# Low weight parts handed on from where they are made, conversions respread, rings of four

## The chip, the cores and the metric

The kernel runs on one core of one Trainium2 chip. The metric is the device time of one execution in microseconds (us). Engines: PE (TensorE), DVE (VectorE), ACT (ScalarE), POOL (GpSimd) and SP, whose queue issues nearly all DMAs. Each engine executes its own instructions in the order in which the program lists them.

## What is computed

Three stages run one after the other; all inputs are float32, but the two weights of the middle stage come to the chip as 64-bit floats.

```python
q_p, k_p = phi(q_s), phi(k_s)                 # attention with random features, 4 x 8 x 576 x 64
kv = einsum('bhsm,bhsd->bhmd', k_p, v);  z = sum(k_p, axis=2)
x = (einsum(q_p, kv) / (einsum(q_p, z) + 1e-6))       # -> 2304 tokens x 512
h = x @ w_in;  g = h / (1 + exp(-1.702 * h));  x = g @ w_out        # MLP, 512 -> 2048 -> 512
# top-1 mixture of 8 experts: out = gate * (relu(x @ w1[e]) @ w2[e]), e = argmax(x @ w_gate)
```

A float32 matmul operand is split in a high and a low part (`hi` rounded by a copy, `lo = x - hi`), and a product is made of three matmuls: high by high, high by low, low by high.

## The kernel before

**Attention.** The 18 tiles of 128 tokens run in a loop over `t` (L390), each iteration with a k tile five ahead and a q tile. `advance` (L319) issues the next load of a fixed sequence `k0 k1 .. k4 k5 q0 k6 q1 ..`; a k load (L200) is followed at once by the load of its v tile (L203), which goes into one of `NV = 5` tiles whose rows hold 65 floats for each head, 64 of them loaded (256 bytes at a time). Two `advance` calls later the tile is squared (L214), and then `proj` multiplies it (L231). `ksums` adds k and v (L257). Before the loop seven matmuls on a tile `warm` keep PE busy.

**MLP.** `steps` (L355) is a list of 80 pairs (block of tokens, f): block 0 with f = 0..7, block 1 with f = 0..15, block 0 with f = 8..15, then blocks 2, 3, 4. In loop iteration n (called step n here), PE does `hmm(n)` (12 matmuls, L439 to L441, with the weights `w_f`), and then `ymm(n-1)` (12 matmuls, L465, L466, L468, with the weights `o_f`). In between `gate(n)` runs on ACT (two gelus, L454 and L455) and DVE (L456). The tail of the attention lies in steps 0 and 1 by the table `DR`: in step 0 `num` and `norm` of the last tile follow `hmm(0)`, and in step 1 `xtr`, a transpose on PE (L308) and a copy on ACT (L309), follows `gate(1)`. After it the PSUM banks of the attention go to the MLP, so `ymm(0)`, at the end of step 1, waits for that copy.

**Conversion.** Each of the 32 weight chunks (`w_0..w_15`, `o_0..o_15`, 512 KB each) is loaded as 64-bit words into a staging tile (`cload`, L132) and turned into float32 by an absolute value on ACT (`cabs`, L139) and four DVE operations (`cops`, L117, L118, L120, L122); `chigh` copies the high part on ACT (L164), which stays in SBUF, and `clow` subtracts it (L172). The low part is stored to DRAM (`cstore`, L156), and every use of it, the first too, fetches it back (`wfetch`, L372, for step n+2; `ofetch`, L378, for step n+1). Low parts live in two rings, `l0` for w and `l1` for o, with three tiles each. The list `order` (L103) sets the order of the chunks: `w0 w1 o0 w2 o1 w3 o2 ..`. By the end of the attention eight chunks are done, with `clow` on POOL. The other 24 are done in the MLP, with `clow` on DVE: `CMLP = (2, 2, 2, 2, 2, 1)` is the number of conversions in steps 0 to 5, with one in each step after that. One "conversion" in the loop is `cabs(1)`, `cpop(4)`, `clow`, `chigh(1)`, `cload(1)` (L739 to L744), a software pipeline: the low part of a chunk is made one conversion after its high part. In the last four steps of each part of a block, `xsplit` (L359) splits the activations of the next part: a copy on ACT (L178) and a subtraction (L179) on DVE, or on POOL once all chunks are converted.

Of the kernel before, what the change touches and what calls it, by code (L numbers as in the profile page):

```python
# [10 lines left out]
F32 = mybir.dt.float32  # L11
F32R = mybir.dt.float32r
BF16 = mybir.dt.bfloat16
# [7 lines left out]
B, H, S, D, M = 4, 8, 576, 64, 128  # L21
NTOK, DM, DFF = 2304, 512, 2048
E, F = 8, 1024
NT = NTOK // 128
KC = DM // 128
NF = DFF // 128
# [3 lines left out]
NT0 = BLOCKS[-2][0]  # L30
# [10 lines left out]
NJ = NTOK // SUB  # L41
# [29 lines left out]
def fused_kernel(ctx: ExitStack, tc: tile.TileContext, qT, kT, vt, omT, w_in, w_out, w_gate, w_gateT, w1, w2, consts, out):  # L71
    nc = tc.nc
# [3 lines left out]
    wts = ctx.enter_context(tc.tile_pool(name="wts", bufs=1))  # L76
# [17 lines left out]
    def winc(f):  # L94
        return win[f // 4][:, f % 4]
# [4 lines left out]

    order = [0] + [c for f in range(NF - 1) for c in (f + 1, NF + f)] + [2 * NF - 1]  # L103
    cnext, cst2, cf32 = [0, 0, 0, 0, 0], [], {}
    for i in range(2):
        w = keep.tile([128, 2, 512, 2], I32, name=f"st{i}", tag=f"wg{i}", bufs=1)
        cst2 += [w[:, 0], w[:, 1]]

    def low(m):
        return wts.tile([128, 512], F32R, name=f"l{m}", tag=f"l{m}", bufs=3)  # L110

    def cops(i):
        t, lo, hi = cf32[i], cst2[i % 4][:, :, 0], cst2[i % 4][:, :, 1]
# [37 lines left out]
    halves, stored = [], []  # L151

    def cstore():

        for c, lo in stored:
            nc.sync.dma_start(out=lod[c], in_=lo.bitcast(F32))  # L156
        stored.clear()
# [10 lines left out]
    def clow(eng):  # L168

        for i, c, hi in halves:  # L170
            lo = low(int(c >= NF))
            eng.tensor_tensor(out=lo, in0=cf32.pop(i), in1=hi.bitcast(F32), op=ALU.subtract)  # L172
            stored.append((c, lo))
            cnext[4] += 1
        halves.clear()

    def split(hi, lo, src, eng):
        nc.scalar.copy(out=hi, in_=src)  # L178
# [5 lines left out]
    kp = kctx.enter_context(tc.tile_pool(name="attk", bufs=1, side="right"))  # L184
# [2 lines left out]
    wkp = qctx.enter_context(tc.tile_pool(name="attps", bufs=1, space=PSUM, side="left"))  # L187
    sp = sctx.enter_context(tc.tile_pool(name="atts", bufs=1, side="left"))
    omx = sp.tile([128, M], F32, name="omx", bufs=1)
    warm = kp.tile([128, 512], BF16, name="warm", bufs=1)  # L190

    NV = 5
    vs = [kp.tile([128, H, D + 1], F32, name=f"v{i}", tag=f"v{i}", bufs=1) for i in range(NV)]
    scale = 1.0 / np.sqrt(np.sqrt(D))
    raws = {}

    def load(kind, t):
        src = qT if kind == "q" else kT
        r = sp.tile([128, H, 128], F32, name="raw", tag="raw", bufs=4)
        nc.sync.dma_start(out=r[0:64].rearrange("p h t -> p (h t)"), in_=src[t])  # L200
        raws[kind, t] = r
        if kind == "k":
            nc.sync.dma_start(out=vs[t % NV][:, :, 0:D], in_=vt[t].rearrange("p (h d) -> p h d", h=H))  # L203


    SQ = (((nc.vector, 0, 4), (nc.scalar, 4, 8)), ((nc.scalar, 0, 8),), ((nc.gpsimd, 0, 6), (nc.vector, 6, 8)), ((nc.gpsimd, 0, 8),))
# [10 lines left out]
    pj, phi = {}, {}  # L217
# [27 lines left out]
    def kvacc(t, parts=(0, 1)):  # L245

        e, v = phi["k", t], vs[t % NV]
        for i, (r, n, b) in enumerate(segments(t)):
# [63 lines left out]
    seq = [("k", t) for t in range(LEAD)]  # L312
# [4 lines left out]
    ln = [0]  # L317

    def advance():  # L319
        if ln[0] < len(seq):  # L320
            load(*seq[ln[0]])
        if 2 <= ln[0] < len(seq) + 2:
            square(*seq[ln[0] - 2])
        ln[0] += 1
# [3 lines left out]
    for i in range(WARM):  # L328
        p = work_bank("wm")
# [22 lines left out]
    xsp, wsp, osp, phs, gsp, pys, ysb = {}, {}, {}, {}, {}, {}, {}  # L352
# [5 lines left out]
    def xsplit(v, k, eng):  # L358
        b = parts[v][0]  # L359
        n = BLOCKS[b][1] * 128  # L360
        xsp[b, k] = [xa.tile([128, 512], F32R, name=f"x{m}", tag=f"x{m}{(v * KC + k) % 6}", bufs=1)[:, 0:n] for m in "hl"]
        split(*xsp[b, k], xT[b][:, k], eng)

    def hilo(m):
        return [wts.tile([128, 512], F32R, name="wh1", tag="cf", bufs=3) if m else
                xb.tile([128, 512], F32R, name="wh0", tag="wh0", bufs=2), low(m)]

    def wfetch(b, f):

        lo = low(0)  # L370
        assert f in order[:cnext[4] - len(stored)]
        nc.sync.dma_start(out=lo.bitcast(F32), in_=lod[f])  # L372
        wsp[b, f] = winc(f).rearrange("p k f -> p (k f)"), lo

    def ofetch(b, f):
        lo = low(1)
        assert NF + f in order[:cnext[4] - len(stored)]
        nc.sync.dma_start(out=lo.bitcast(F32), in_=lod[NF + f])  # L378
        osp[b, f] = woutc(f), lo

# [9 lines left out]
    for t in range(NT):  # L390
        k = t + LEAD
        if t >= 2:
            norm(t - 2)
        if k < NT:
            proj("k", k)
            expo("k", k)
            advance()
        if t >= 1:
            qtr(t - 1)
        cpop(1)  # L400
        if k - 1 < NT:
            ksums(k - 1)
        if k == NT:
            kctx.close()
            xa = ctx.enter_context(tc.tile_pool(name="xa", bufs=1, side="right"))
            php = ctx.enter_context(tc.tile_pool(name="ph", bufs=1, space=PSUM, side="right"))
        proj("q", t)
        expo("q", t)
        cstore()
        cabs(1)  # L410
        clow(nc.gpsimd)
        advance()
        if k >= NT:
            advance()
        if t >= 1:
            num(t - 1)
        if t >= 2:
            xtr(t - 2)
        cpop(1)
        chigh(1)  # L420
        cload(1)
        for i in XSL.get(t, ()):
            xsplit(0, i, nc.gpsimd)
        if t >= NT - 3:
            (lambda: wfetch(0, 0), lambda: wfetch(0, 1), lambda: ofetch(0, 0))[t - NT + 3]()
    norm(NT - 2)
    sctx.close()


    xb = ctx.enter_context(tc.tile_pool(name="xb", bufs=1, side="right"))  # L430

    def hmm(b, f):
# [62 lines left out]
        del pys[b]  # L495

    def logit(b, j, e):
        junk = sb.tile([128, DM], F32, name="junk", tag="junk", bufs=1)
        t = BLOCKS[b][0] + j
        nc.vector.tensor_tensor_reduce(out=junk, in0=ysb[b][j], in1=wg[e // 4][:, e % 4], scale=1.0, scalar=0.0,  # L500
                                       op0=ALU.mult, op1=ALU.add, accum_out=lg[:, t, e:e + 1])
# [27 lines left out]
    def small(name, *shape):  # L529
        return sb.tile([128, *shape], F32, name=name, tag=name, bufs=1)  # L530
# [49 lines left out]
    def place(t0, nb):  # L580

        c = slice(t0, t0 + nb)
        v = small("pv", NT0, E)[:, 0:nb]
        jc = small("pj", NT0, NJ)[:, 0:nb]
        q = small("pq", NT0)[:, 0:nb]
        r = small("pr", NT0)[:, 0:nb]
        nc.vector.tensor_tensor(out=v, in0=oh[:, c], in1=bc(oh0, nb, 1), op=ALU.mult)
        nc.vector.tensor_reduce(out=inr[:, c], in_=v, axis=AX.X, op=ALU.add)

        nc.vector.scalar_tensor_tensor(out=q, in0=rank[:, c], scalar=n0[:, 0:1], in1=inr[:, c], op0=ALU.is_ge, op1=ALU.mult)  # L590
        nc.vector.scalar_tensor_tensor(out=r, in0=q, scalar=n0[:, 1:2], in1=rank[:, c], op0=ALU.mult, op1=ALU.add)

        nc.vector.tensor_tensor(out=inr[:, c], in0=q, in1=inr[:, c], op=ALU.subtract)
        nc.vector.tensor_scalar_add(inr[:, c], inr[:, c], 1.0)
        nc.vector.tensor_tensor(out=jc, in0=bc(r, NJ, 2), in1=bc(cst[:, C_J:C_J + NJ], nb, 1), op=ALU.is_ge)
        nc.vector.tensor_reduce(out=jf[:, c], in_=jc, axis=AX.X, op=ALU.add)
        nc.vector.tensor_scalar_add(jf[:, c], jf[:, c], -1.0)
        nc.vector.scalar_tensor_tensor(out=slot[:, c], in0=jf[:, c], scalar=-float(SUB), in1=r, op0=ALU.mult, op1=ALU.add)
# [80 lines left out]
    def esplit(i, f, m):  # L679
        spl[i, f, m] = hilo(m)  # L680
        split(*spl[i, f, m], ew[i % 2][f // 4 * 2 + m][:, f % 4 * 512:(f % 4 + 1) * 512], nc.vector)

    def drain(n, h):
        for c, t in DR.get((n, h), ()):
            dict(q=qtr, n=num, d=norm, x=xtr)[c](NT + t)
# [5 lines left out]
    for n in range(len(steps) + 1):  # L691
        if n < len(steps):
            b, f = steps[n]
            cstore()
            if n + 2 < len(steps):
                wfetch(*steps[n + 2])
            if n + 1 < len(steps):
                ofetch(*steps[n + 1])
            else:
                for m in range(2):  # L700
                    esplit(0, 0, m)
            drain(n, 0)
            hmm(b, f)
            gate(b, f)
            drain(n, 1)
            if n == 1:
                qctx.close()
                sb = ctx.enter_context(tc.tile_pool(name="sb", bufs=1, side="left"))
                ps = ctx.enter_context(tc.tile_pool(name="ps", bufs=1, space=PSUM, side="left"))
                wgT = sb.tile([128, KC, E], F32, name="wgT", bufs=1)  # L710
                lg = sb.tile([128, NT, E], F32, name="lg", bufs=1)
                mx = sb.tile([128, NT], F32, name="mx", bufs=1)
# [25 lines left out]
            if cnext[4] < len(order):  # L738
                for i in range(CMLP[n] if n < len(CMLP) else 1):  # L739
                    cabs(1)  # L740
# [4 lines left out]
            if (b, f) == (0, HF):  # L745
                assert cnext[4] == len(order)
                for i in range(2):
                    wg.append(keep.tile([128, 4, DM], F32, name=f"wg{i}", tag=f"wg{i}", bufs=1))
                    nc.sync.dma_start(out=wg[i].rearrange("p e d -> p (e d)"),
                                      in_=w_gate[4 * i:4 * i + 4].rearrange("(o e) d -> o (e d)", o=1).to_broadcast([128, 4 * DM]))  # L750
# [23 lines left out]
        if n < len(steps):  # L774
            v = next(v for v, (i, f0, f1) in enumerate(parts) if i == b and f0 <= f < f1)
# [247 lines left out]
    nb = nc.values_load(ctl[0:1, 2, 0:1], min_val=0, max_val=MAXB)  # L1023
# [11 lines left out]

HF = 8

CMLP = (2, 2, 2, 2, 2, 1)

XSL = {NT - 5: (0,), NT - 4: (1,), NT - 3: (2,), NT - 2: (3,)}  # L1040
DR = {(0, 0): (("x", -2), ("q", -1)), (0, 1): (("n", -1), ("d", -1)), (1, 1): (("x", -1),)}
# [46 lines left out]
```

## Time and profile before

| | us |
|---|---|
| median of 3 runs (lowest to highest) | 801.73 (800.62 to 803.67) |
| the profiled execution, whole | 800.57 |
| its span, first to last instruction | 798.8 |
| busy: PE, DVE, ACT, POOL | 770.1, 482.5, 372.1, 159.2 |

The span holds the attention (up to 146 us), the MLP (to 547 us) and the experts. PE is busy 96% of the span, with a mean granted clock of 0.99. In the profile a matmul is counted as busy until its modelled end, and matmuls overlap, so a stretch in which PE is wholly busy can still be slower than another: the number of matmuls in a stretch tells it. An instruction's idle time in brackets is what its engine waited just before it, and for whom.

### The profile page before, as it was taken

How to read it: one execution, taken by the hardware profiler on the slowest of the kernel's cores; microseconds unless marked ns; L12 is line 12 of the kernel's file. 1: busy time of each engine (PE TensorE's matmuls, PEld its weight loads, DVE VectorE, ACT ScalarE, POOL GpSimd, SP SyncE). 2: the span in 40 equal slices, each digit the busy share in tenths (PEclk: the TensorE clock that was granted, in tenths of full speed). 3: DMA queues.
4: the chain of work that ended last, by engine and by line, in shares of the span. 5: the costliest groups of instructions: out<-in, count | busy, mean ns of one | idle time of the engine just before them, and what ended most of it. 6: DMA issues, size and time to landing. Idle time of an engine off the chain costs nothing.

```text
span 798.8 us, 16225 instructions
## 1 busy us (share of the span) xinstructions
PE 770.1 (96%) x6257; PEld 693.3 (87%) x6257; DVE 482.5 (60%) x1075; ACT 372.1 (47%) x873; POOL 159.2 (20%) x129
## 2 busy tenths in 40 slices
PE   6999999799999999999999999999999999999994
PEld 5889998587888888888889989988999999999993
DVE  3687877589655138756317744743787656556551
ACT  5689889645543232221222223124354655555551
POOL 3576646200000111100010011000015502321011
PEclk9999999999999999999999999999999999999997
DMA  9967554399874463633335445983076555654011
GB/s 213 202 148 185 140 141 149 112 276 317 297 256 155 133 247 106 199 95 102 97 89 185 131 120 181 345 276 124 2 272 221 204 179 206 219 187 143 24 31 33
DMA packets 66020, 134.62 MB, mean 169 GB/s; under 512 B 24784, under 2 KB 24848, under 8 KB 61584
## 3 DMA queue, kind: packets, MB, share of 16 engines
q1 hardware_dynamic: 62784, 124.04, 51.0%
q0 software_dynamic: 3072, 9.44, 4.0%
q8 instruction: 51, 0.84, 0.4%
q14 instruction: 33, 0.27, 0.1%
q10 hardware_dynamic: 80, 0.03, 0.0%
HBM read 118.81 MB, written 18.87 MB: 172 GB/s over the span
## 4 chain that ended last, share of the span: by engine, by line
PE 61%; issue 22%; POOL 6%; DVE 4%; DMA 3%; ACT 2%; SPq 0%; POOLq 0%; DVEq 0%; ACTq 0%
PE py L465 8%; PE py L466 8%; PE py L468 8%; PE ph L441 8%; PE ph L439 8%; PE ph L440 7%; PE pj L231 6%; POOL out L848 2%; POOL yg L633 2%; PE kv L257 2%; PE nu L293 2%; PE tr L283 2%; DMA lod<-l 1%; PE xt L308 1%; DMA raw<-qT 1%
## 5 line engine op out<-in xcount | busy, mean ns | idle before, releaser
L454 ACT ACTIVATE gh<-ph 128x512 fp32r<-128x512 f32 (+1 forms) x80 | 44.4, 555 | 232.0 <-PE ph L441 232.0
L456 DVE TENSOR_TENSOR gl<-sg,gh 128x512 fp32r<-128x512 f32 (+1 forms) x80 | 51.0, 638 | 160.0 <-ACT sg L455 153.1
L439 PE MATMUL ph<-xh,win 128*128 128x512 f32 (+1 forms) x320 | 118.8, 371 | 0.0
L441 PE MATMUL ph<-xh,l 128*128 128x512 f32 (+1 forms) x320 | 118.2, 369 | 0.6 <-DMA l<-lod 0.6
L440 PE MATMUL ph<-xl,win 128*128 128x512 f32 (+1 forms) x320 | 117.9, 368 | 0.3 <-DVE xl L179 0.3
L465 PE MATMUL py<-wo,gh 128*128 128x512 f32 x288 | 113.5, 394 | 4.6 <-ACT big L309 4.6
L466 PE MATMUL py<-l,gh 128*128 128x512 f32 x288 | 113.3, 393 | 0.0
L500 DVE CUSTOM_DVE_ANT_0 junk<-ysb,wg 128x512 f32<-128x512 f32 x120 | 87.0, 725 | 3.1
L179 POOL TENSOR_TENSOR xl<-big,xh 128x512 fp32r<-128x512 f32 (+1 forms) x20 | 24.5, 1225 | 316.4 <-PE py L466 166.7
L468 PE MATMUL py<-wo,gl 128*128 128x512 f32 x288 | 78.7, 390 | 0.0
L231 PE MATMUL pj<-omx,raw 128*64 128x128 f32 x1152 | 69.9, 275 | 4.8 <-POOL raw L214 3.1
L214 POOL TENSOR_TENSOR raw<-raw 64x1024 f32<-64x1024 f32 (+1 forms) x34 | 66.4, 1958 | 36.0 <-DMA raw<-kT 15.3
L821 PE MATMUL oT<-gh,wh 128*128 128x288 f32 x256 | 71.9, 304 | 0.0
L805 PE MATMUL ph<-yhl,wh 128*128 128x288 f32 x256 | 71.8, 303 | 0.0
L822 PE MATMUL oT<-gh,l 128*128 128x288 f32 x256 | 70.0, 296 | 0.0
L806 PE MATMUL ph<-yhl,wh 128*128 128x288 f32 x256 | 69.9, 295 | 0.0
L231 PEld LDWEIGHTS pj<-omx,raw 128*64 128x64 f32 x1152 | 62.2, 137 | 8.6 <-issue 3.9
L440 PEld LDWEIGHTS ph<-xl,win 128*128 128x128 f32 x320 | 60.1, 188 | 9.3 <-DVE xl L179 0.8
L465 PEld LDWEIGHTS py<-wo,gh 128*128 128x128 f32 x288 | 54.5, 189 | 15.3 <-ACT big L309 4.9
L441 PEld LDWEIGHTS ph<-xh,l 128*128 128x128 f32 x320 | 60.1, 188 | 8.8 <-DMA l<-lod 1.4
L439 PEld LDWEIGHTS ph<-xh,win 128*128 128x128 f32 x320 | 60.1, 188 | 8.4
L238 DVE TENSOR_REDUCE nm<-pj 128x4 f32<-128x512 f32 x72 | 48.7, 688 | 30.6 <-PE pj L231 21.3
(178 smaller groups left out, 1439.0 us busy)
## 6 DMA issues: line engine op xcount, KB each, us to landing
l<-lod SPq DMA_DIRECT2D x160, 256.0 KB, 2.8
f<-w SPq DMA_DIRECT2D x20, 1024.0 KB, 6.3
e<-w SPq DMA_DIRECT2D x16, 1024.0 KB, 7.1
st<-w_in SPq DMA_DIRECT2D x16, 512.0 KB, 4.9
st<-w_out SPq DMA_DIRECT2D x16, 512.0 KB, 5.7
lod<-l SPq DMA_DIRECT2D x32, 256.0 KB, 3.2
yd<-ysb SPq DMA_DIRECT2D x22, 256.0 KB, 2.4
raw<-kT SPq DMA_DIRECT2D x18, 256.0 KB, 3.8
```

The lines of the kernel that those rows point to most:

```text
L231: nc.tensor.matmul(p[c:c + 64, j], r[:, 4 * g + j, c:c + 64], omx, start=True, stop=True)
L439: nc.tensor.matmul(p, wh[:, c], xh, start=k == 0, stop=False)
L440: nc.tensor.matmul(p, wh[:, c], xl, start=False, stop=False)
L441: nc.tensor.matmul(p, wl[:, c], xh, start=False, stop=k == KC - 1)
L465: nc.tensor.matmul(p, gh[:, c], wh, start=(b, f) in pfirst, stop=False)
L466: nc.tensor.matmul(p, gh[:, c], wl, start=False, stop=False)
L468: nc.tensor.matmul(p, gl[:, j * 128:(j + 1) * 128], wh, start=False, stop=(b, f) in plast)
L500: nc.vector.tensor_tensor_reduce(out=junk, in0=ysb[b][j], in1=wg[e // 4][:, e % 4], scale=1.0, scalar=0.0, op0=ALU.mult, op1=ALU.add, accu ...
L805: nc.tensor.matmul(p, wh[:, w], yh[:, k], start=k == 0, stop=False)
L806: nc.tensor.matmul(p, wh[:, w], yl[:, k], start=False, stop=False)
L821: nc.tensor.matmul(p, wh[:, w], hh, start=f == 0, stop=False)
L822: nc.tensor.matmul(p, wl[:, w], hh, start=False, stop=False)
```

## The change

- `low` rings have four tiles instead of three.
- `order` swaps one pair: `o7` comes before `w8`, so that all that the first part needs comes first.
- `CMLP = (0, 2, 2)`: no conversion in step 0, two in steps 1 and 2, then one a step.
- `direct`: a fetch for a chunk whose low part was made in this step or the one before, or is not made yet, is left out; the use takes the tile in which `clow` makes it. The store to DRAM stays, for later blocks. With the counters of the code followed by hand, this leaves out 14 of the 160 fetches: o3 to o7, w5 to w7, then o12 to o15, w14 and w15.
- `cstore` comes behind the two fetches of a step, no longer ahead of them.
- In the attention a v tile is loaded one `advance` later than its k tile (so behind the next k or q load), into one of four tiles; `warm` takes a tile of the ring `phik`.
- To make room, tiles move: x4 and x5 to a pool `xa2`, `wh0` to a pool `xc`, `junk` and the larger `pj` to the ring `cf`.

```diff
-    order = [0] + [c for f in range(NF - 1) for c in (f + 1, NF + f)] + [2 * NF - 1]
+    order = [0] + [c for f in range(NF - 1) for c in ((f + 1, NF + f) if f + 1 != HF else (NF + f, f + 1))] + [2 * NF - 1]
...
-        return wts.tile([128, 512], F32R, name=f"l{m}", tag=f"l{m}", bufs=3)
+        return wts.tile([128, 512], F32R, name=f"l{m}", tag=f"l{m}", bufs=4)
...
             stored.append((c, lo))
+            made[c] = at[0]
+            fresh[c] = lo
+            if c in wanted:
+                take(c, *wanted.pop(c))
...
+    def take(c, b, f):
+        (wsp if c < NF else osp)[b, f] = winc(c).rearrange("p k f -> p (k f)") if c < NF else woutc(c - NF), fresh[c]
+
+    def direct(c, b, f):
+        if made.get(c, at[0]) <= at[0] - 2:
+            return False
+        if c in fresh:
+            take(c, b, f)
+        else:
+            wanted[c] = b, f
+        return True
...
-    NV = 5
+    NV = 4
...
-        if kind == "k":
-            nc.sync.dma_start(out=vs[t % NV][:, :, 0:D], in_=vt[t].rearrange("p (h d) -> p h d", h=H))
+
+    def vload(t):
+        nc.sync.dma_start(out=vs[t % NV][:, :, 0:D], in_=vt[t].rearrange("p (h d) -> p h d", h=H))
...
             load(*seq[ln[0]])
+        if ln[0] <= len(seq) and seq[ln[0] - 1][0] == "k":
+            vload(seq[ln[0] - 1][1])
...
     def wfetch(b, f):
 
+        if direct(f, b, f):
+            return
         lo = low(0)
...
             b, f = steps[n]
-            cstore()
+            at[0] = n
             if n + 2 < len(steps):
                 wfetch(*steps[n + 2])
...
+            cstore()
             drain(n, 0)
             hmm(b, f)
...
-CMLP = (2, 2, 2, 2, 2, 1)
+CMLP = (0, 2, 2)
```

## Rows read from the trace of the kernel before

**Rows 1.** Waits of PE, whole span: us in total, times, longest.

```profile
PE py L465 <- ACT big L309: 4.6, 1, 4.6
```

**Rows 2.** Stretches: us, busy us (instructions) per engine, granted clock, DMA share, GB/s.

```profile
0.00:20.00 20.00, 13.87 (x233) 10.96 (x233) 6.75 (x11) 11.65 (x35) 6.58 (x14) 1.00 1.08 213
...
150.00:158.50 8.50, 3.77 (x22) 2.58 (x16) 6.66 (x16) 4.71 (x9) 1.09 (x5) 0.97 0.32 94
158.50:162.50 4.00, 3.91 (x11) 3.14 (x12) 3.92 (x8) 1.87 (x4) 0.00 (x0) 0.63 0.77 242
162.50:203.00 40.50, 39.58 (x172) 31.80 (x172) 34.22 (x63) 21.95 (x40) 0.00 (x0) 1.00 0.94 302
203.00:300.00 97.00, 97.00 (x430) 80.34 (x429) 45.95 (x84) 35.26 (x64) 5.15 (x4) 1.00 0.65 214
```

**Rows 3.** Timeline, steps 0 and 1: start, us, engine, line, what [idle before].

```profile
152.70 0.39 PE L441 MATMUL ph<-xh,l 128*128 128x512 f32 x1
...
153.27 0.68 PE L308 MATMUL xt<-cst,xn 128*128 128x128 f32 x4 [0.18 <-DVE xn L302]
...
156.46 0.62 ACT L164 CAST win<-cf 128x512 fp32r<-128x512 f32 x1 [1.75 <-DVE cf L122]
...
156.98 0.59 ACT L454 ACTIVATE gh<-ph 128x512 fp32r<-128x512 f32 x1
...
157.47 0.59 ACT L455 ACTIVATE sg<-ph 128x512 f32<-128x512 f32 x1
...
157.95 0.59 ACT L309 COPY big<-xt 128x512 f32<-128x512 f32 x1
...
158.59 0.79 PE L465 MATMUL py<-wo,gh 128*128 128x512 f32 x1 [4.64 <-ACT big L309]
...
161.63 0.39 PE L466 MATMUL py<-l,gh 128*128 128x512 f32 x1
```

**Rows 4.** Groups of DVE instructions, 155 to 262 us: busy us, mean ns.

```profile
L120 DVE SCALAR_TENSOR_TENSOR cf<-st,cf 128x512 int32<-128x512 int32 x23 | 16.0, 698 | 0.8
L122 DVE SCALAR_TENSOR_TENSOR cf<-st,cf 128x512 int32<-128x512 int32 x23 | 15.7, 684 | 0.0
...
L456 DVE TENSOR_TENSOR gl<-sg,gh 128x512 fp32r<-128x512 f32 x19 | 13.1, 690 | 26.5 <-ACT sg L455 26.5
...
L118 DVE TENSOR_SCALAR cf<-cf 128x512 int32<-128x512 int32 x22 | 9.4, 428 | 0.8
L117 DVE TENSOR_SCALAR cf<-cf 128x512 f32<-128x512 f32 x22 | 9.3, 421 | 0.8 <-ACT cf L139 0.8
L172 DVE TENSOR_TENSOR l<-cf,wo 128x512 fp32r<-128x512 f32 x13 | 8.9, 685 | 0.0
```

**Rows 5.** Timeline, step 6: a fetch of a low part and its reader.

```profile
180.99 0.38 SPq L372 DMA_DIRECT2D l<-lod  x1
...
185.75 0.50 PE L441 MATMUL ph<-xh,l 128*128 128x512 f32 x1 [0.57 <-DMA l<-lod]
```

**Rows 6.** Timeline, step 7 and the beginning of step 8.

```profile
190.87 0.39 PE L439 MATMUL ph<-xh,win 128*128 128x512 f32 x1
...
198.03 0.68 DVE L172 TENSOR_TENSOR l<-cf,win 128x512 fp32r<-128x512 f32 x1
...
199.36 0.50 PE L440 MATMUL ph<-xl,win 128*128 128x512 f32 x1 [0.35 <-DVE xl L179]
```

**Rows 7.** DMA, first 20 us: packets; v loads (count, KB, us to landing).

```profile
DMA packets 7128, 4.25 MB, mean 213 GB/s; under 512 B 6360, under 2 KB 6424, under 8 KB 7126
...
v<-vt SPq DMA_DIRECT2D x7, 256.0 KB, 7.0
```

**Rows 8.** Timeline, first k tiles: projection on PE and square on POOL.

```profile
15.14 1.97 PE L231 MATMUL pj<-omx,raw 128*64 128x128 f32 x32 [1.01 <-POOL raw L214]
...
18.03 1.89 POOL L214 TENSOR_TENSOR raw<-raw 64x1024 f32<-64x1024 f32 x1 [2.94 <-ACT phik L240]
...
19.97 1.97 PE L231 MATMUL pj<-omx,raw 128*64 128x128 f32 x32 [1.93 <-POOL raw L214]
```

More of the change, by code (lines that the diff above doesn't have):

```diff
@@ L173, in clow @@
             stored.append((c, lo))
+            made[c] = at[0]
+            fresh[c] = lo
+            if c in wanted:
+                take(c, *wanted.pop(c))
             cnext[4] += 1
         halves.clear()
+    at, made, fresh, wanted = [-9], {}, {}, {}
+    def take(c, b, f):
[8 more added lines that the diff above has]
+        return True
     def split(hi, lo, src, eng):
@@ L189, in fused_kernel @@
     omx = sp.tile([128, M], F32, name="omx", bufs=1)
-    warm = kp.tile([128, 512], BF16, name="warm", bufs=1)
-    NV = 5
+    warm = kp.tile([128, 512], BF16, name="warm", tag="phik", bufs=3)
+    NV = 4
     vs = [kp.tile([128, H, D + 1], F32, name=f"v{i}", tag=f"v{i}", bufs=1) for i in range(NV)]
@@ L360, in xsplit @@
         n = BLOCKS[b][1] * 128
-        xsp[b, k] = [xa.tile([128, 512], F32R, name=f"x{m}", tag=f"x{m}{(v * KC + k) % 6}", bufs=1)[:, 0:n] for m in "hl"]
+        i = (v * KC + k) % 6
+        xsp[b, k] = [(xa if i < 4 else xa2).tile([128, 512], F32R, name=f"x{m}", tag=f"x{m}{i}", bufs=1)[:, 0:n] for m in "hl"]
         split(*xsp[b, k], xT[b][:, k], eng)
@@ L365, in hilo @@
         return [wts.tile([128, 512], F32R, name="wh1", tag="cf", bufs=3) if m else
-                xb.tile([128, 512], F32R, name="wh0", tag="wh0", bufs=2), low(m)]
+                xc.tile([128, 512], F32R, name="wh0", tag="wh0", bufs=2), low(m)]
     def wfetch(b, f):
+        if direct(f, b, f):
+            return
         lo = low(0)
-        assert f in order[:cnext[4] - len(stored)]
         nc.sync.dma_start(out=lo.bitcast(F32), in_=lod[f])
@@ L375, in ofetch @@
     def ofetch(b, f):
+        if direct(NF + f, b, f):
+            return
         lo = low(1)
-        assert NF + f in order[:cnext[4] - len(stored)]
         nc.sync.dma_start(out=lo.bitcast(F32), in_=lod[NF + f])
@@ L424, in fused_kernel @@
         if t >= NT - 3:
+            at[0] = -1
             (lambda: wfetch(0, 0), lambda: wfetch(0, 1), lambda: ofetch(0, 0))[t - NT + 3]()
@@ L427, in fused_kernel @@
     sctx.close()
+    xa2 = ctx.enter_context(tc.tile_pool(name="xa2", bufs=1, side="right"))
     xb = ctx.enter_context(tc.tile_pool(name="xb", bufs=1, side="right"))
@@ L497, in logit @@
     def logit(b, j, e):
-        junk = sb.tile([128, DM], F32, name="junk", tag="junk", bufs=1)
+        junk = wts.tile([128, DM], F32, name="junk", tag="cf", bufs=3)
         t = BLOCKS[b][0] + j
@@ L583, in place @@
         v = small("pv", NT0, E)[:, 0:nb]
-        jc = small("pj", NT0, NJ)[:, 0:nb]
+        if t0:
+            jc = small("pj", 3, NJ)[:, 0:nb]
+        else:
+            jc = wts.tile([128, nb, NJ], F32, name="pj", tag="cf", bufs=3)
         q = small("pq", NT0)[:, 0:nb]
@@ L709, in fused_kernel @@
                 ps = ctx.enter_context(tc.tile_pool(name="ps", bufs=1, space=PSUM, side="left"))
+                xc = ctx.enter_context(tc.tile_pool(name="xc", bufs=1, side="right"))
                 wgT = sb.tile([128, KC, E], F32, name="wgT", bufs=1)
```

## The prediction

> **What bounds the kernel now.** I read the waits of PE first. The longest single wait of the whole run is one of 4.6 us, of the first matmul of `ymm(0)` for the copy `big` on ACT [rows 1]. The next longest are waits for squares of k tiles, 1.01 and 1.93 us [rows 8]. Next come the stretches [rows 2]: see there how many matmuls PE does, not only how long it is busy. From 203 to 300 us it does 430 in 97 us, which is 0.226 us each and 5.4 us for a step of 24: PE never waits, and nothing that is taken off another engine can help there. From 150 to 158.5 us it is busy for 3.77 of 8.50 us. From 158.5 to 162.5 us the granted clock is 0.63, so part of this stretch ran at 1.2 and not at 2.4 GHz, right after the idle time. From 162.5 to 203 us PE loses 0.92 us of busy time, with the DMA share at 0.94. In the first 20 us it is busy for 13.87. So what can be won lies at two places: the passage from attention to MLP, and the first 20 us. Then I read the timeline there, from the late instruction backwards [rows 3, 8].
>
> **Step 1, the conversions taken out of step 0.** `hmm(1)` ends at 153.1 us (152.70 + 0.39), and then its gelu could run on ACT. It starts at 156.98. Ahead of it in ACT's queue stand the casts of the two conversions of step 0, the second at 156.46 after 1.75 us of waiting for DVE's L122 [rows 3]. The second gelu and the copy follow at 157.47 and 157.95, and PE starts at 158.59, 1.61 us after the first gelu. With no conversion in step 0, nothing on ACT stands between the gelus of step 0 and those of step 1. The first gelu then starts at about 153.2, and PE at 153.2 + 1.6 = 154.8 us, so **3.8 us** earlier. What is late next is the same chain, two gelus and the copy, which leaves PE about 0.9 us of idle time behind the transpose that began at 153.27. The most that this wait can give is its 4.64 us; the least, with the chain as it is in the rows, 3.8.
>
> **The clock behind it.** From 158.59 to 161.63 us seven matmuls start, 0.434 us each [rows 3]; at 0.226 they take 1.6 us and not 3.0. So the low clock costs **1.5 us**. In the first 20 us PE has waits of 1.01 and 1.93 us before matmuls [rows 8], and the granted clock is 1.00 all through [rows 2]. The wait that is left is of that size, so I take the whole 1.5 us as won. Bounds: 0 (the clock falls all the same) to 1.5.
>
> **The conversions themselves** are as many as before, 24. One costs DVE 0.42 + 0.43 + 0.70 + 0.68 + 0.69 = 2.9 us, and the gate's subtraction adds 0.69 [rows 4]. With two conversions a step DVE needs 6.5 us, more than PE's 5.4; with one 3.6, and 4.3 where an `xsplit` adds another subtraction. Steps 1 and 2 thus put DVE 2.2 us behind, step 3 takes back 1.8, step 4 the rest. The cover of these 2.2 us is that `gl` is read a step later, and that the low part made in step 1 (`o3`) is read in step 4, those of step 2 (`w5`, `o4`) in step 5. Cost: nothing; without that cover PE would wait for what is left of the 2.2 us, once. Before, steps 0 to 4 had two each, and DVE was busy for 34.2 of 40.5 us [rows 2]. The conversions end about three steps later, with `o15` in step 23, one step ahead of its use. Three of the `xsplit` subtractions of steps 20 to 23 go from POOL to DVE thereby; DVE is busy less than half of 203 to 300 us [rows 2], which hides them.
>
> **Fetches left out, `cstore` moved, rings of four.** In step 6 the fetch of `w6` is issued at 180.99 us, behind two stores on SP, and its reader on PE waits 0.57 us for it, to 185.75 [rows 5]. `w6` is now taken from where it is made, so this wait goes: **0.6 us** (bounds 0 and 0.6). The other 13 fetches left out hold up no matmul today, so they give nothing in themselves; the room in the DMA queues (share 0.94, [rows 2]) is a cover, not a gain. Fetches that come ahead of `cstore` on SP no longer wait behind a low part of DVE. What is queued behind them, stores and loads of staging tiles, is needed a step or more later. The ring's waits fall on DVE's L172 and on SP; L172 to `wo` idles 0.0 us today with three tiles [rows 4], so I expect none with four.
>
> The other small wait, 0.35 us before 199.36, is for the subtraction of `xsplit` in step 7 [rows 6], which stands at the end of DVE's work of that step: gate, conversion, low part, `xsplit`. All four are still there. Gain: 0 (bounds 0 and 0.4).
>
> **The front: v behind the next k.** The wait before the projection of k4, 1.93 us before 19.97, ends with the square on POOL that starts at 18.03 [rows 8]. The profile puts its start down to ACT's exponentials, but the square reads only the loaded tile, so it is the load that came last. The DMA engines have a share of 1.08 all through the first 20 us [rows 2], so a load lands when the bytes ahead of it have moved. In the new order one v load of 256 KB fewer stands ahead of k3 and k4. By bytes, at 213 GB/s [rows 2, 7], that is 1.2 us. The upper bound: at the rate of 162.5 to 203 us (302 GB/s at 0.94) the first 20 us would have carried 6.9 MB and not 4.25; the difference is 8.3 us of transfer time at that rate, and if the seven v loads [rows 7] cost all of it, one costs 0.8 + 1.2 = 2.0 us. The lower bound is 0, if SP or the tile of the ring holds k4 back. I take **1.2 us**, the row's own rate.
>
> Weighed against a rule: 6360 of 7128 packets in the first 20 us are under 512 B [rows 7], and the v tiles are what is loaded in pieces of 256 B. The Trainium skill ("DMA: Bandwidth & Descriptors", Specifications) gives 512 B as the least transfer for line rate, and has a read-modify-write below it. By that rule the v load is dearer than its bytes, the 2.0 us would be nearer than the 1.2, and the sum 0.8 us better. The rows agree that the rate is low here, but do not part v from the rest, so the sum keeps the rate.
>
> **Sum.** 3.8 + 1.5 + 0.6 + 0 + 1.2 = 7.1 us. Behind these places PE is the bound up to the end, so the gains stay. The profiled execution took 800.57 us and would take 793.5; the median of the runs is 801.73, 1.2 above, and I predict for that median: 801.73 - 7.1 = **794.6 us**. With the bounds the forecast's own range is 801.73 - (3.8 + 0 + 0.6 + 0) = 797.3 to 801.73 - (4.6 + 1.5 + 0.6 + 0.4 + 2.0) = 792.6.
>
> **Rivals.**
>
> *A. The wait in step 1 stays.* `ymm(0)` could wait for something that ends hardly sooner than the copy does now, such as a tile in the rearranged pools, and the clock falls as before. Then only 0.6 + 1.2 are won: 799.9 us. For it: a wait is put down to the last of several releasers, so the second to last is not seen. Against it: the chain of gelus, copy and PE has no gap of its own from 156.46 on [rows 3].
>
> *B. The front loses.* v is asked for half an iteration later, and behind a k or q load that itself waits for its tile; a v load took 7.0 us to land [rows 7]. If `ksums` waits for v once for half of that, 3.5 us, and the 1.2 us are not won, the time is 794.6 + 4.7 = 799.3 us. For it: DMA share 1.08. Against it: by the code v is read two to three iterations after its new request, and the tile it takes (one of four) has had its last reader earlier in the same iteration, ahead of the projection for which SP waits anyway. The Trainium skill ("DMA: Bandwidth & Descriptors", Rules for kernel authors) says to issue a DMA early and wait late; this change issues v later, and by that rule B would come.
>
> *C. Slower: a low part made too late.* `o6`, `o7`, `o14` and `o15` are now read by `ymm` in the step after the one in which DVE makes them. In step 7 such a part was begun at 198.03 and ended 7.8 us after the step's first matmul at 190.87 [rows 6]; its reader in the next step, the fourteenth matmul, is due 5.4 + 13 x 0.226 = 8.3 us after. The spare time is 0.5 us. If DVE is a step's work (4.3 us) behind at all four, PE loses 4 x 3.8 = 15.2 us: 809.8. It decides against the change from a lateness of 0.5 + 7.1 / 4 = 2.3 us. For it: DVE is 2.2 us behind after step 2. Against it: it catches up by step 4, and a stall of PE gives DVE time, so four in full are hardly possible.
>
> **Chances.** Forecast 0.70, A 0.12, B 0.10, C 0.08. A measurement of this kernel can tell about 0.5% (4.0 us) from no change, so the border lies at 797.7 and 805.7 us. The forecast's range is wholly faster; A is within; of B 0.03 falls faster and 0.07 within; of C 0.06 is slower and 0.02 within. Faster 0.73, same 0.21, slower 0.06. The range runs from 792.0, just past the forecast's good end, to 800.5, which takes in A and B and leaves out C.
>
> **What would show it.** In the profile after: the wait of PE for `big` is about 1 us, and PE does `ymm(0)` at a granted clock near 1.00; no wait of L441 for a fetch around step 6; a wait of about 0.4 us for `xl` at the beginning of step 8 as before; the projection of k4 starts 1 to 2 us earlier; 146 fetches, and DMA share well under 0.94 in the first ten steps. The prediction is wrong if PE waits in `ymm(6)` or `ymm(7)` for DVE's L172 (C), if L257 waits for v (B), or if the matmuls of `ymm(0)` still take 0.43 us (A, or the term of the clock).

## The result and the profile after

The changed kernel takes 792.57 us (median of 4 runs, 792.30 to 793.07), the kernel before 801.38 us beside it; the ratio is 0.9886, with a 95% interval of [0.9865, 0.9907], so it is faster. Forecast were 794.6 us in a range of 792.0 to 800.5, and a chance of 0.73 for faster. Of the profiled executions, the one after took 793.07 us with a span of 791.3 us, 7.5 us less than that of before.

Waits of PE after, as in [rows 1] (columns as there):

```profile
PE pj L251 <- DVE raw L234: 1.6, 1, 1.6
...
PE py L492 <- ACT big L329: 0.8, 1, 0.8
...
PE ph L467 <- DVE xl L198: 0.3, 1, 0.3
```

The wait for `big` is 0.8 us and not 4.6; the wait for a fetch is gone; the one for `xl` is still there. The trace counts 146 fetches of low parts.

The stretches of [rows 2] after (columns as there):

```profile
0.00:20.00 20.00, 16.10 (x251) 13.71 (x253) 6.81 (x11) 11.76 (x35) 6.68 (x14) 1.00 1.07 205
...
150.00:158.50 8.50, 7.53 (x34) 5.75 (x33) 7.00 (x16) 3.77 (x7) 1.64 (x5) 1.00 0.30 80
158.50:162.50 4.00, 4.00 (x19) 3.32 (x18) 2.30 (x5) 2.25 (x4) 0.00 (x0) 1.00 0.58 226
162.50:203.00 40.50, 40.19 (x178) 32.98 (x177) 31.19 (x56) 20.25 (x37) 0.00 (x0) 1.00 0.68 224
203.00:300.00 97.00, 97.00 (x430) 80.36 (x429) 58.77 (x113) 37.59 (x67) 1.28 (x1) 1.00 0.64 218
```

See the granted clock: 1.00 in the stretch from 158.5 us, where it was 0.63, and 1.00 in the stretch ahead of it, where it was 0.97. From 162.5 to 203 us PE starts 178 matmuls instead of 172, and the DMA share is 0.68 instead of 0.94. From 203 us on the rate is the old one, 430 matmuls in 97 us. The passage itself, as in [rows 3] (timeline: start, us, engine, line, what, idle before):

```profile
152.00 0.60 ACT L481 ACTIVATE gh<-ph 128x512 fp32r<-128x512 f32 x1 [1.62 <-PE ph L468]
...
152.50 0.59 ACT L482 ACTIVATE sg<-ph 128x512 f32<-128x512 f32 x1
...
152.97 0.59 ACT L329 COPY big<-xt 128x512 f32<-128x512 f32 x1
...
153.62 0.50 PE L492 MATMUL py<-wo,gh 128*128 128x512 f32 x1 [0.79 <-ACT big L329]
...
155.34 0.39 PE L493 MATMUL py<-l,gh 128*128 128x512 f32 x1
```

The gelus of step 1 start as soon as `hmm(1)` is done, the copy `big` follows, PE starts 0.65 us after it, and the eighth matmul of `ymm(0)` starts 1.72 us after the first, where it took 3.04.

### The profile page after: what moved, and what is told of

Read it like the earlier page. It is cut to its first block, busy times and chain, and to the rows that moved or that the text cites. A ratio compares the mean times of both kernels' runs of the same rounds, so it can differ in the third digit from the quotient of the medians.

```text
span 791.3 us, 16189 instructions
## 1 busy us (share of the span) xinstructions
PE 769.9 (97%) x6257; PEld 694.3 (88%) x6257; DVE 477.3 (60%) x1078; ACT 372.1 (47%) x873; POOL 156.5 (20%) x125
## 4 chain that ended last, share of the span: by engine, by line
PE 69%; issue 19%; POOL 5%; DVE 3%; DMA 2%; ACT 2%; POOLq 0%; DVEq 0%; ACTq 0%; SPq 0%
PE ph L466 8%; PE ph L467 8%; PE ph L468 8%; PE py L492 8%; PE py L493 8%; PE py L495 8%; PE pj L251 7%; PE kv L277 2%; PE tr L303 2%; POOL out L880 2%; PE nu L313 2%; POOL yg L663 2%; DMA raw<-kT 1%; PE xt L328 1%; PE ph L837 1%
## 5 line engine op out<-in xcount | busy, mean ns | idle before, releaser
L198 POOL TENSOR_TENSOR xl<-big,xh 128x512 fp32r<-128x512 f32 (+1 forms) x17 | 21.4, 1259 | 312.6 <-ACT xh L197 251.8
L527 DVE CUSTOM_DVE_ANT_0 junk<-ysb,wg 128x512 f32<-128x512 f32 x120 | 80.0, 722 | 0.0
L251 PE MATMUL pj<-omx,raw 128*64 128x128 f32 x1152 | 71.7, 279 | 2.5 <-DVE raw L234 1.6
L251 PEld LDWEIGHTS pj<-omx,raw 128*64 128x64 f32 x1152 | 64.1, 140 | 6.1 <-issue 3.8
L495 PEld LDWEIGHTS py<-wo,gl 128*128 128x128 f32 x288 | 54.1, 188 | 11.6
```

The costliest lines, as they stand in the source:

```text
L251: nc.tensor.matmul(p[c:c + 64, j], r[:, 4 * g + j, c:c + 64], omx, start=True, stop=True)
L495: nc.tensor.matmul(p, gl[:, j * 128:(j + 1) * 128], wh, start=False, stop=(b, f) in plast)
```

## The experiments

Each kernel was timed beside the kernel before on its chip; a ratio is to that kernel, with its 95% interval.

**e1: only step 0 freed.** The kernel before, with nothing changed but the numbers of conversions.

```diff
-CMLP = (2, 2, 2, 2, 2, 1)
+CMLP = (0, 2, 2, 2, 2, 2, 1)
```

> The kernel before with one edit: no conversion in step 0, two in each of steps 1 to 5, every low part still stored and fetched, three tiles in a ring. My theory (the casts of step 0 hold up the gelus of step 1 and the copy that ymm(0) waits for, and the clock falls behind that wait): the first matmul of step 2 starts 5.2 us earlier than in the kernel before (162.8 to about 157.6 us), 3.8 from the wait and 1.4 from the clock; the time falls by 4 to 5 us, to about 797, less whatever late fetches take back. Rival 1 (the low parts must be used where they are made, or the gain is lost to fetches that now come a step later): PE waits for fetches in steps 4 to 7 for more than 3 us in all, and the time is 799 or more. Rival 2 (something else ends as late as the copy): the wait in step 1 stays above 4 us, time 801.

Measured: 805.55 us, ratio 1.0052 [1.0032, 1.0071]: 0.5% **slower** than before, with an interval clear of 1. Its waits of PE:

```profile
PE ph L441 <- DMA l<-lod: 8.0, 3, 3.5
...
PE py L465 <- ACT big L309: 0.8, 1, 0.8
```

The wait for `big` falls to 0.8 us just as in the changed kernel, so rival 2 is out. But 8.0 us of waits for fetches come instead: rival 1. The chain of waits of e1 shows where they are from (start, us, what):

```profile
170.24 0.61 DVE l L172
...
171.89 8.17 DMA lod<-l
...
180.13 2.66 DMA l<-lod
```

A low part is made, its store takes 8.2 us to land, SP waits for that before it may issue the fetch of the same part, and the fetch takes 2.7 us more; PE waits until it lands. The second wait, 1.0 us for the fetch of w7, is of the same kind. The third, 3.5 us in step 8, is not: its fetch is of w0, whose low part was stored long before, and takes 8.9 us from issue to landing right behind the stores of step 6. The granted clock falls behind these waits, to 0.91 on average from 162.5 to 203 us. Steps 6 to 8 take 13.3 us more than three undisturbed steps of 5.44 us, where it is 1.8 us in the kernel before. SP's own waits between 162 and 204 us say the same (us in total, times, longest):

```profile
SPq L372 <- DMA lod<-l: 14.5, 3, 6.9
SPq L378 <- DMA lod<-l: 8.0, 3, 7.4
```

While SP stands there, the loads of the next chunks (L132) stand behind it; what that costs the conversions was not measured apart. In the kernel before, the two conversions of step 0 bought a lead that hides store and fetch but for one small wait.

**e4: the whole change, but all low parts fetched.**

```diff
     def direct(c, b, f):
-        if made.get(c, at[0]) <= at[0] - 2:
-            return False
+        return False
...
-CMLP = (0, 2, 2)
+CMLP = (0, 2, 2, 2, 2, 2, 1)
...
             at[0] = n
+            cstore()
             if n + 2 < len(steps):
```

(the later `cstore()` is taken out)

> The changed kernel with direct use off: every low part is stored and fetched, the store ahead of the fetches as in the kernel before, conversions 0, 2, 2, 2, 2, 2, then 1 a step so that each is stored in time; rings of four, later v loads, moved tiles stay. My theory: the gains at the front and in step 1 (1.1 + 5.2 us) stay, and of the 1.2 us that the changed kernel won between steps 2 and 8 a part is lost; time 793 to 794.5. Rival (direct use is needed to keep what step 1 gains): waits of PE for fetches of 3 us or more in steps 4 to 8, time 796 or more.

Measured: 805.90 us, ratio 1.0054 [1.0033, 1.0075]. The rival (796 or more) again; my theory (793 to 794.5) missed by more than 11 us. PE waits 9.1 us for fetches:

```profile
PE ph L467 <- DMA l<-lod: 9.1, 3, 6.3
```

Behind the longest of them, 6.3 us, the clock falls as well; the mean of 162.5 to 203 us is 0.87:

```profile
162.50:203.00 40.50, 32.07 (x126) 25.12 (x125) 31.54 (x59) 18.81 (x33) 0.00 (x0) 0.87 0.68 211
```

PE starts 126 matmuls there instead of 178. The four tiles do not help: what is late is above all the path store, landing, fetch. So with step 0 free, direct use is worth 805.9 - 792.6 = 13.3 us, together with the place of `cstore` and the smaller number of conversions in steps 3 to 5, which changed with it here.

**e2: the whole change, but conversions in step 0 again.**

```diff
-CMLP = (0, 2, 2)
+CMLP = (2, 2, 2, 2, 2, 1)
```

> The changed kernel with one edit: the old numbers of conversions a step (2, 2, 2, 2, 2, 1, then 1), so two in step 0 again; direct use, rings of four, later v loads and moved tiles stay. My theory: the wait of ymm(0) is back at about 4.6 us and the clock falls to the lower level behind it; the time is 5.2 us above the changed kernel, about 798. Rival (direct use and the rings of four bring the gain, the step 0 matters little): within 1.5 us of the changed kernel, 792 to 794.

Measured: 798.63 us, ratio 0.9959 [0.9944, 0.9974], 6.1 us above the changed kernel. The wait is back, and the clock with it:

```profile
159.44 0.79 PE L492 MATMUL py<-wo,gh 128*128 128x512 f32 x1 [4.64 <-ACT big L329]
...
162.59 0.63 PE L493 MATMUL py<-l,gh 128*128 128x512 f32 x1
...
164.72 0.60 PE L466 MATMUL ph<-xh,win 128*128 128x512 f32 x1
```

```profile
158.50:162.50 4.00, 3.06 (x7) 2.48 (x8) 3.93 (x8) 2.19 (x4) 0.00 (x0) 0.50 0.85 312
162.50:203.00 40.50, 39.93 (x171) 32.52 (x170) 33.78 (x62) 22.13 (x39) 0.00 (x0) 0.97 0.90 299
```

(first the timeline, then the stretches). The theory holds, with a bit more than its 5.2 us: here the eighth matmul starts 3.15 us after the first, close to the 3.04 of before, but the lower clock goes on into the next `hmm`: its first matmul, at 164.72, still takes 0.60 us and not 0.39.

**e5: my rival C, made to happen.** One conversion fewer in step 2 makes four low parts in the very step that reads them.

```diff
-CMLP = (0, 2, 2)
+CMLP = (0, 2, 1)
```

> The changed kernel with one edit: one conversion in step 2 instead of two, so that o6, o7, o14 and o15 are made on DVE in the very step whose ymm reads them (this is my rival C, made to happen). Theory (DVE ends such a part 7.8 us after the step's first matmul, its reader is due 2.95 us after): ymm(6) and ymm(7) wait 4.9 us each for L172, ymm(14) about 3 and ymm(15) about 2.4 us; the clock falls behind the longer ones, 1.4 us each; in all 15 to 18 us, so 808 to 811. Rival (a stall of PE gives DVE the time to catch up, so only the first costs): 5 to 7 us, 798 to 800.

Measured: 818.50 us, ratio 1.0203 [1.0170, 1.0236]; 7.5 us beyond the 808 to 811 of my theory. The waits (totals, then three of them in the timeline with what ended them):

```profile
PE py L493 <- DVE l L172: 14.2, 4, 4.5
PE ph L468 <- DVE l L172: 3.0, 2, 1.5
```

```profile
187.58 0.50 PE L468 MATMUL ph<-xh,l 128*128 128x512 f32 x1 [1.52 <-DVE l L172]
...
194.83 0.56 PE L493 MATMUL py<-l,gh 128*128 128x512 f32 x1 [4.46 <-DVE l L172]
...
206.61 0.80 PE L493 MATMUL py<-l,gh 128*128 128x512 f32 x1 [4.46 <-DVE l L172]
```

The four waits that I named are there: 4.46, 4.46, 2.94 and 2.34 us, 14.2 in all (I had worked out 4.9, 4.9, 3 and 2.4, in all 15.2). The second is as long as the first, so the stall of PE did not let DVE catch up. The likely reason, not tested, is that DVE's work of the step hangs on the gelu of that step. I had missed w7 and w15, whose readers, at the start of the next `hmm`, wait 1.5 us each: 3.0. The waits make 17.2 of the 25.9 us over the changed kernel. Nearly all the rest lies in the same steps: steps 7 to 9, 23 and 24 together are 24.2 us longer than in the changed kernel. The granted clock is 0.89 from 185 to 200 us and 0.72 from 200 to 212, against 1.00 in the changed kernel, so the lower clock has a share in the rest that is not worked out. So the slack of direct use is real and small: at one conversion less all the gain and more is lost.

**e7: three tiles in the rings.**

```diff
-        return wts.tile([128, 512], F32R, name=f"l{m}", tag=f"l{m}", bufs=4)
+        return wts.tile([128, 512], F32R, name=f"l{m}", tag=f"l{m}", bufs=3)
```

> The changed kernel with three tiles in each ring of low parts, as in the kernel before. My theory (direct use, not the fourth tile, takes the fetches off the path): no wait of PE comes back, 792 to 793.2. Rival (a part that is used where it is made holds its tile from step n-2 to its use, so three tiles block DVE's L172 or SP): waits of PE or of DVE's L172 of 1 us or more in steps 3 to 10, time 794 or more.

Measured: 793.38 us, ratio 0.9899 [0.9866, 0.9932], and no wait in the MLP that the changed kernel lacks. The fourth tile shows no effect.

**e3: only v later.** The kernel before, with `vload` behind the next `load` as in the change, and five v tiles.

```diff
-        if kind == "k":
+
+    def vload(t):
+        if True:
             nc.sync.dma_start(out=vs[t % NV][:, :, 0:D], in_=vt[t].rearrange("p (h d) -> p h d", h=H))
...
             load(*seq[ln[0]])
+        if ln[0] <= len(seq) and seq[ln[0] - 1][0] == "k":
+            vload(seq[ln[0] - 1][1])
```

> The kernel before with one edit: each v tile is loaded one advance later than its k tile (five v tiles as before). My theory (a v load fewer stands ahead of k3 and k4 in a full DMA queue): the projection of k4 starts 1 to 2 us earlier than 19.97 us, the first matmul of the MLP about 1.1 us earlier than 146.1, time about 800.2. Rival (the gain at the front came from the smaller ring of v tiles, the shared warm tile or chance): the first matmul of the MLP at 146.1 +- 0.3, time 801.4.

Measured: 799.66 us, ratio 0.9975 [0.9960, 0.9990], some 2 us faster. In its trace k4 is projected at 18.55 us, the MLP's first matmul is at 145.04 and the transpose of step 1 starts at 152.23: the theory, against the first trace of before. But e1, with the front as it was, has that first matmul at 145.46 and e12 (below), the kernel before, at 144.50, so one trace does not tell the two fronts apart.

**e9: the change without its front and without the fourth tile.**

```diff
-    NV = 4
+    NV = 5
...
             load(*seq[ln[0]])
-        if ln[0] <= len(seq) and seq[ln[0] - 1][0] == "k":
-            vload(seq[ln[0] - 1][1])
+            if seq[ln[0]][0] == "k":
+                vload(seq[ln[0]][1])
...
     load(*seq[0])
+    vload(0)
```

(with three tiles in the rings, as in e7)

> The changed kernel without its front and without the fourth tile: v loads right behind their k loads into five v tiles, three tiles in the rings of low parts; direct use, the new order and the new numbers of conversions stay. Theory from the runs so far (direct use lets the conversions leave step 0 at no price; the later v loads give about 2 us on their own): about 2 us above the changed kernel, 794 to 795.5. Rival (the front does nothing, its 2 us in the run with v alone were chance): as the changed kernel, 792 to 793.3.

Measured: 793.10 us, ratio 0.9892 [0.9873, 0.9912], in the rival's range and not in my theory's; beside it the changed kernel once more:

**e11: the changed kernel again**, no edit.

> The changed kernel as it is, beside the two others on the same chip: 792 to 793.5 by the runs so far.

Measured: 792.31 us, ratio 0.9878 [0.9859, 0.9896]. Between e9 and e11 lie 0.8 us, less than either interval is wide. e3 and e9 do not agree on the front: alone it gave some 2 us, in the whole change it can't be told from nothing. The place of `cstore`, the swap of `o7` and `w8` and the moved tiles are still in e9, and no run tries any of them alone.

**e12: the kernel before again**, one run, for a second trace of it.

> The kernel before as it is, for a second trace of it. In its first trace 7 matmuls behind the wait of ymm(0) ran at the lower clock (1.4 us lost), in the two experiments that keep that wait (e2, e3) about 12 (2.5 us). If the length of the low clock changes from run to run: between 7 and 12 here, and the time from ymm(0) to the first expert matmul between 395.3 and 396.4 us; the front (transpose in step 1) anywhere from 152 to 154 us, as in the kernels with later v loads. If the first trace is the rule for this kernel: 7 matmuls and 395.3 us, transpose at 153.3.

Measured: 799.91 us. The first matmul of its `ymm(0)`, the eighth, and the first one behind the lower clock, in the `hmm` that follows:

```profile
157.01 0.79 PE L465 MATMUL py<-wo,gh 128*128 128x512 f32 x1 [4.64 <-ACT big L309]
...
160.17 0.63 PE L466 MATMUL py<-l,gh 128*128 128x512 f32 x1
...
163.15 0.41 PE L441 MATMUL ph<-xh,l 128*128 128x512 f32 x1
```

```profile
150.00:158.50 8.50, 3.67 (x15) 2.53 (x14) 8.24 (x18) 4.16 (x8) 1.09 (x5) 0.87 0.45 152
158.50:162.50 4.00, 4.00 (x11) 3.13 (x10) 3.64 (x8) 1.54 (x3) 0.00 (x0) 0.50 0.79 200
162.50:203.00 40.50, 39.01 (x170) 31.49 (x169) 32.74 (x60) 21.02 (x38) 0.00 (x0) 0.99 0.90 295
```

The clock is 0.50 in all of 158.5 to 162.5 us, and 0.87 before it: the low clock is there at the first matmul, at 157.01, and reaches to about 163.15, some 6.1 us and fourteen matmuls instead of the 3.0 us and seven of the first trace. The waits of e2 and e3 are followed by 0.50 in that stretch too. So the size of this loss changes from run to run, and by more than I had expected: fourteen matmuls lie outside my 7 to 12, the 397.2 us from `ymm(0)` to the experts outside 395.3 to 396.4, and the transpose at 151.69 outside 152 to 154.

**e6 and e8: a front with less DMA.** In e6 the ones that follow each head of v come with v from DRAM, so that a v load moves one piece of 2080 bytes a partition.

```diff
-        nc.sync.dma_start(out=vs[t % NV][:, :, 0:D], in_=vt[t].rearrange("p (h d) -> p h d", h=H))
+        nc.sync.dma_start(out=vs[t % NV].rearrange("p h d -> p (h d)"), in_=vt[t])
...
-    for v in vs:
-        nc.gpsimd.memset(v[:, :, D:D + 1], 1.0)
...
-        vt=np.ascontiguousarray(v.transpose(0, 2, 1, 3)).reshape(NT, 128, H * D),
+        vt=np.ascontiguousarray(np.pad(v.transpose(0, 2, 1, 3), ((0, 0), (0, 0), (0, 0), (0, 1)), constant_values=1.0)).reshape(NT, 128, H * (D + 1)),
```

> The changed kernel with one edit: the column of ones that follows the 64 floats of each head of v comes with v from DRAM, so a v load moves one piece of 2080 bytes a partition and not eight of 256 (266 KB instead of 262 KB), and the memsets of ones go. If a v load costs what its bytes cost (the 1.2 us of my sum): no change, 792 to 793, and the projection of k4 as in the changed kernel. If small pieces make it dear (2.0 us a load, the page's rule on transfers under 512 bytes): three v loads ahead of k4 are 1.2 us cheaper each, the DMA share of the first 60 us falls, k4 is projected 1 to 2 us earlier, time 790.5 to 791.7.

Measured: 791.90 us, ratio 0.9876 [0.9843, 0.9909], between the two forecasts and not to be told from the changed kernel's. But the DMA queues are relieved (the front's stretches):

```profile
0.00:20.00 20.00, 16.52 (x303) 14.01 (x305) 8.89 (x13) 12.81 (x40) 8.75 (x11) 1.00 0.93 246
20.00:60.00 40.00, 38.45 (x754) 35.08 (x752) 30.69 (x52) 33.19 (x111) 24.34 (x14) 1.00 0.65 179
```

From 20 to 60 us the share falls from the changed kernel's 0.94 at 186 GB/s to 0.65 at 179 GB/s, and k4 is projected at 16.89 us (18.91 in the changed kernel). So the small pieces do cost DMA time. These rows agree with the rule of the Trainium skill ("DMA: Bandwidth & Descriptors", Specifications) that transfers under 512 bytes miss the line rate; the read-modify-write that it names no run here shows. PE turns little of it into time.

In e8 the first staging load is issued at another place in the front: behind q0 instead of ahead of k3 (the expectation says k6, which is one load further).

```diff
     for t in range(3):
-        if t >= 2:
-            cload(1)
         advance()
...
-        if t >= LEAD - 2:
+        if t >= LEAD - 3:
             cload(1)
```

> As e6_v_rows, and the first load of a staging tile (512 KB) comes behind the load of k6 instead of ahead of k3. If the front goes at the pace of the DMA bytes ahead of k3 and k4: 512 KB at 205 GB/s are 2.6 us, of which PE can use 1 to 2 before it is bound by its own chain; 1 to 2 us below e6_v_rows. Rival (behind the first loads PE, ACT and DVE pace the front, not DMA): within 0.5 us of e6_v_rows.

Measured: 790.13 us, ratio 0.9871 [0.9829, 0.9914], four runs from 788.2 to 795.0, so it was run again, as **e10**:

> The kernel with v loaded in whole rows and the first staging load behind k6, once more and beside the changed kernel on the same chip, since its four runs spread from 788 to 795. If the front is DMA-paced in the changed kernel: 2 to 3 us below the changed kernel. Rival: within 1 us of it.

Measured: 791.25 us, ratio 0.9868 [0.9848, 0.9888], beside e11's 0.9878. It is the fastest that was run, but it is 1.1 us below the changed kernel beside it, nearer to the rival than to the 2 to 3 us of the theory, and the intervals do not part the two. In its two traces the transpose of step 1 starts at 148.19 (e8) and 150.40 us (e10), ahead of all other kernels here.

## Why the prediction was right, and where its sizes were off

One table for the kernels that bear on the sum. Column 1 is the start of the transpose of step 1, which ends the front and all of the attention; column 2 the first matmul of `ymm(0)`; column 3 the first matmul of the experts, which follows the last one of the MLP at once (so the MLP ends there, and not at 547 us as said ahead). Each is from one trace.

| kernel | transpose | ymm(0) | experts | from transpose to experts |
|---|---|---|---|---|
| before | 153.27 | 158.59 | 553.87 | 400.60 |
| before again (e12) | 151.69 | 157.01 | 554.18 | 402.49 |
| v later (e3) | 152.23 | 157.55 | 553.92 | 401.69 |
| changed, step 0 full (e2) | 154.11 | 159.44 | 555.09 | 400.98 |
| changed | 152.15 | 153.62 | 546.36 | 394.21 |
| changed again (e11) | 152.55 | 154.03 | 546.77 | 394.22 |
| direct only (e9) | 152.45 | 153.92 | 546.67 | 394.22 |
| three tiles (e7) | 151.35 | 152.82 | 545.56 | 394.21 |

**The wait in step 1: 3.8 us predicted, 3.85 measured** (4.64 to 0.79). The chain behind the transpose is as I read it off [rows 3], in e1 too, where only this was changed.

**The clock: 1.5 us predicted.** Between this pair of traces it is 3.04 - 1.72 = 1.3 us. In e12 fourteen matmuls run at the low clock and take 163.15 - 157.01 = 6.1 us; the same fourteen take 3.3 us in the changed kernel, so 2.8 us are lost. This term was sized from one trace, one in which the clock rose early. That is also the likely reason why the medians differ by 8.8 us and the two profiled executions by 7.5; it is argued from the traces of before, e2, e3 and e12, not shown for each run.

**Fetches left out: 0.6 us predicted, 1.2 measured.** From the first matmul of step 2 to the wait for `xl` in step 8 the kernel before took 199.36 - 162.78 = 36.6 us, the changed one 191.85 - 156.47 = 35.4. Of the 1.2 us, 0.9 lie in step 6, whose length is 6.31 us instead of 5.44, and 0.3 in step 7. The wait of 0.57 us thus cost 0.87; the other short waits, 1.18 and 0.72 us below and 0.31 for `xl`, lengthen their steps by 0.3 us more than the wait too. In step 7 the reader of w7's fetch starts 0.34 us after the matmul ahead of it, and not 0.23 (kernel before):

```profile
191.10 0.39 PE L440 MATMUL ph<-xl,win 128*128 128x512 f32 x1
191.44 0.50 PE L441 MATMUL ph<-xh,l 128*128 128x512 f32 x1
```

So it was not true that "the other 13 fetches left out hold up no matmul today". In e12 and e3 it is w7's fetch that PE waits for, 1.18 and 0.72 us, and w6's costs next to nothing.

And here the working had a gap that did not cost it the result: I priced direct use alone, at 0.6, and the freed step 0 alone, at 5.3, and added. By e1 the second alone makes the kernel slower, by 3.7 us, and e4 bears it out. I wrote of the fetches that "they give nothing in themselves"; as soon as step 0 is freed, those of w6 and w7 hold PE up for 4.5 us in e1, and w0's, issued behind such stores, for 3.5. My sum holds only for both together.

**The front: 1.2 us predicted.** The pair of traces has just this: k4 at 18.91 instead of 19.97, and the transpose 1.1 us earlier. The earlier k4 is borne out by the other traces: it is projected at 19.35 to 20.10 us in the four with the front as it was (before, e12, e1, e9) and at 17.25 to 19.44 in the seven with the new one (changed, e11, e2, e3, e4, e5, e7). But it is not seen at the end of the front: the transpose lies between 151.69 and 153.27 in those four and between 151.35 and 154.11 in those seven. So the step that the sum took for granted, that what k4 wins stays won up to the end, is not borne out. The end of the front moves by 2 us and more from run to run; what moves it is not shown, and in e6, with the DMA share down to 0.65 from 20 to 60 us, the transpose (151.48) lies in the same span. By the medians, e3 says that v later gives 2 us alone, e9 that it gives none that can be seen in the whole. How much it gives stays open. (The upper bound of 2.0 us in the working mixes two rates: at the 347 GB/s that give its 6.9 MB in 20 us, one v load comes to 1.9.)

**The wait for `xl`** stayed, 0.31 us against 0.35, as predicted. The conversions end in step 23 as predicted, but four steps later than before (step 19), not three; PE waits for none of them. **Rival A** is out by the row of 0.79 us. **Rival B** is out: no wait of PE for a v load is in the list. **Rival C** did not come, and e5 shows that it stood one conversion away. Its waits have the size that was worked out (14.2 us against 15.2), but its price is 25.9 us, since the readers of w7 and w15 and what follows the waits, the lower clock among it, were not in it.

From the transpose to the experts the gain is 6.4 us by the first trace of before and 8.3 us by the second, where 5.9 was predicted. In the first that is 3.85 for the wait, 1.3 for the clock and 1.2 for the fetches, and with the front's 1.1 it makes up the 7.5 us between the two traces; in the second it is 3.85, 2.8 and 1.5. The medians differ by 8.8 us, not 7.1, and 792.57 lies at the good end of the forecast's own range (792.6). So the places and the main term were right, the fetches were priced too low, the clock's loss changes from run to run, and the front's gain is not shown to reach the end. That the sum came as near as 2 us is in part luck, since these errors have opposite signs.

## What to carry to other kernels

Before work is moved later in a pipeline, follow every product of it to its reader through memory: in e1 a part that went to DRAM and back needed 8.2 + 2.7 us, and the early work that looked misplaced was what had paid for that. Two edits that each look like a gain, or like nothing, are to be tried apart and together; here one alone made the kernel slower. And PE lost 1.3 to 2.8 us more behind its wait of 4.64 us, so a stall ahead of a long run of matmuls is to be priced with the clock behind it, from more than one trace.

## What was not expected of the hardware

After a stall of the same 4.64 us, the lower clock held for 3.0 us of matmuls in one trace and for 6.1 us in another of the same kernel; after 0.79 us at the same place it did not fall in any. Short waits of PE (0.31 to 1.18 us) each lengthened its step by 0.3 us more than the wait. A store of 256 KB to DRAM that lands in 2.0 us at best took 8.2 us in e1: the DMA share was 0.87 to 0.95 from its issue at 171.89 to 177 us, and fell to 0.09 in its last microsecond.
